# Column tiles for the token tails, and scores in two row-tiled groups behind a fence

## The chip, the cores and the metric

The kernel runs on one core of a Trainium2 chip. Its engines: TensorE (PE, its weight loads PEld) for matmuls, VectorE (DVE), ScalarE (ACT) and GpSimd (POOL) for the rest; PSUM is the memory, in banks, that the matmuls write. The metric is the device time in microseconds (us), a median of several executions; the spans in the profiles are some 1.8 us shorter.

## The reference

Eight batches of 576 tokens. First attention over pooled keys and values: keys and values are averaged over 8 neighbours (72 remain), 8 heads of 64. Then a mixer over tokens and one over channels:

```python
scores = scale * np.matmul(q, k_p.transpose(0, 1, 3, 2))      # per batch and head: 576 x 72
attn = softmax(scores);  x = attn @ v_p                        # 576 x 512 per batch, heads side by side
h = np.maximum(x.T @ w_tok1, 0.0) @ w_tok2                     # token mixer, 576 -> 256 -> 576
u = x + h.T
out = u + np.maximum(u @ w_ch1, 0.0) @ w_ch2                   # channel mixer, 512 -> 1536 -> 512
```

## The kernel before

All batches share one stream of instructions. The two excerpts below are abridged. "Unit n" is the channel mixer of batch n (lines 512 and 534, 24 steps each of two 128x512 matmuls). Step plans, one dictionary per unit, insert the other stages between these steps: `>s0` at step 22 is the first score stage of batch n+2.

576 tokens are 4 x 128 and a tail of 64. The tails of two batches are joined to a ninth "tile" of 128 rows and go through the channel mixer in a last unit, the tail unit. The second token-mixer stage for a joined tail took four full matmuls, with weights padded with zeros, so that each batch's tail falls in its own half of the rows:

```python
if c < 4:
    mms = [(w_tok2[:, m, c * P:(c + 1) * P], st["AT"][:, m, :]) for m in range(2)]
else:                                                   # u4: w_tok2t is half zeros
    mms = [(w_tok2t[:, m, half, :], tails[b // 2, half][:, m, :]) for half in range(2) for m in range(2)]
for i, (w, a) in enumerate(mms):
    nc.tensor.matmul(out=ps, lhsT=w, rhs=a, start=(i == 0), stop=(i == len(mms) - 1))
```

Scores contract over 64 dimensions, cut into two halves (`db`) of 32 rows, so four heads sit in the four 32-row groups of the array and run at once. A batch has two groups of four heads (`g`). It took three stages: `s0` and `s1`, the first 512 tokens of each group, and `s2`, the last 64 tokens of both:

```python
def score4(gs, n0, n):
    pss = [ps_two.tile([P, 2, 512], FP32) for _ in range(2)]         # four PSUM banks, one per row group
    for i, g in enumerate(gs):
        for db in range(2):
            for l in range(4):
                nc.tensor.matmul(out=pss[l // 2][0:SP, l % 2, i * n:(i + 1) * n], lhsT=kD[quad l, g, db],
                                 rhs=qD[quad l, g, db, n0:n0 + n], tile_position=(l * 32, 0), ...)
    # then two exponentials on ACT, PSUM -> ex
```

The kernel's PSUM pools take eight banks: four in `ps_two` (two buffers of two), three in `ps_one`, one in `ps_tr` ("pt").

The softmax here doesn't subtract the row's maximum and nothing guards it: scores larger than these inputs give would overflow.

## Time and profile before

| | |
|---|---|
| time | 275.05 us (274.76 to 275.32) |
| span of the profiled run | 272.9 us, granted clock 0.997 |
| TensorE busy | 97% |
| ACT, DVE, POOL busy | 40%, 52%, 48% |
| four-head score stage, 512 tokens, first start to next plain matmul | 0.56 us where it waits for nothing (eight of the ten in batches 3 to 7; the others 0.63 and 0.81) |
| tail score stage, 64 tokens, two groups | 0.26 us (four of the five in batches 3 to 7; the other 0.31) |
| tail's second stage | 0.86 us, four times |

How to read it: on a stream that is never idle, only the distance between starts tells what something costs.

### The profile page before, as it was taken

How to read it: one execution, taken by the hardware profiler on the slowest of the kernel's cores; microseconds unless marked ns; L12 is line 12 of the kernel's file. 1: busy time of each engine (PE TensorE's matmuls, PEld its weight loads, DVE VectorE, ACT ScalarE, POOL GpSimd, SP SyncE). 2: the span in 40 equal slices, each digit the busy share in tenths (PEclk: the TensorE clock that was granted, in tenths of full speed). 3: DMA queues.
4: the chain of work that ended last, by engine and by line, in shares of the span. 5: the costliest groups of instructions: out<-in, count | busy, mean ns of one | idle time of the engine just before them, and what ended most of it. 6: DMA issues, size and time to landing. Idle time of an engine off the chain costs nothing.

```text
span 272.9 us, 4515 instructions
## 1 busy us (share of the span) xinstructions
PE 265.5 (97%) x1812; PEld 129.5 (47%) x1812; DVE 142.8 (52%) x280; ACT 110.4 (40%) x182; POOL 131.2 (48%) x121
## 2 busy tenths in 40 slices
PE   8899999999999999999999999999999999999994
PEld 3774545544453544444445444544454444444443
DVE  5487777862674754776266627662765061022022
ACT  2443790058306535425632483147413603603600
POOL 8585221999996995998099999400000000000000
PEclk9999999999999999999999999999999999999998
DMA  7999999995649957993389463214223624024024
GB/s 140 199 202 206 206 205 208 207 202 97 101 63 164 208 107 157 172 211 107 79 144 220 129 115 74 62 59 118 59 58 96 130 58 103 0 57 99 2 49 105
DMA packets 40149, 33.99 MB, mean 125 GB/s; under 512 B 16960, under 2 KB 33600, under 8 KB 40128
## 3 DMA queue, kind: packets, MB, share of 16 engines
q0 software_dynamic: 18672, 17.64, 41.2%
q1 hardware_dynamic: 21296, 15.93, 23.5%
q8 instruction: 14, 0.23, 0.3%
q10 hardware_dynamic: 160, 0.13, 0.2%
q14 instruction: 7, 0.06, 0.1%
HBM read 38.86 MB, written 12.45 MB: 188 GB/s over the span
## 4 chain that ended last, share of the span: by engine, by line
PE 91%; ACT 3%; DMA 2%; DVE 2%; issue 1%; POOL 0%; POOLq 0%
PE p L534 33%; PE p L512 32%; PE p L410 6%; PE p L395 6%; PE p L344 3%; PE p L260 3%; DMA kr<-in_k_dram 2%; ACT ex L265 1%; ACT GT L516 1%; PE p L226 1%; PE p L546 1%; PE pt L420 1%; PE p L204 1%; PE pt L376 1%; PE p L461 0%
## 5 line engine op out<-in xcount | busy, mean ns | idle before, releaser
L534 PE MATMUL p<-w_ch,GT 128*128 128x512 bf16 x420 | 101.2, 379 | 0.0
L512 PE MATMUL p<-uT,w_ch 128*128 128x512 bf16 x384 | 92.4, 379 | 0.1
L516 ACT ACTIVATE GT<-p 128x512 bf16<-128x512 f32 x108 | 63.8, 598 | 70.3 <-PE p L512 69.9
L512 PEld LDWEIGHTS <-w_ch 128*128 128x128 bf16 x432 | 40.7, 98 | 48.2 <-issue 2.7
L534 PEld LDWEIGHTS <-GT 128*128 128x128 bf16 x420 | 38.0, 98 | 42.1 <-issue 3.1
L520 DVE TENSOR_TENSOR o<-p,u 128x512 f32<-128x512 f32 x32 | 21.9, 684 | 33.4 <-PE p L534 33.3
L265 ACT ACTIVATE ex<-p 72x1024 bf16<-72x1024 f32 (+1 forms) x42 | 31.7, 807 | 13.5 <-PE p L260 13.5
L147 POOL TENSOR_TENSOR t<-t 72x512 f32<-72x512 f32 x24 | 30.3, 1264 | 1.9
L146 POOL TENSOR_TENSOR t<-kr 72x1024 f32<-72x1024 bf16 x12 | 25.5, 2125 | 7.6 <-DMA kr<-in_k_dram 6.9
L411 DVE TENSOR_TENSOR u<-p,x 128x512 bf16<-128x512 f32 x32 | 21.6, 688 | 13.7 <-PE p L410 13.4
L146 POOL TENSOR_TENSOR t<-vr 72x1024 f32<-72x1024 bf16 x12 | 25.5, 2125 | 0.8
L442 DVE STREAM_TRANSPOSE uT<-v 128x512 bf16<-128x512 bf16 x20 | 13.0, 686 | 23.9 <-DMA v<-mem 23.9
L248 DVE STREAM_TRANSPOSE qD<-qb 128x576 bf16<-128x576 bf16 x28 | 20.6, 794 | 0.0
L362 DVE TENSOR_TENSOR x<-p,den 128x512 bf16<-128x512 f32 x28 | 19.4, 691 | 1.0
L410 PE MATMUL p<-AT,w_tok 128*128 128x512 bf16 x64 | 18.3, 379 | 0.2 <-ACT GT L516 0.2
L344 PEld LDWEIGHTS <-ex 72*128 72x128 bf16 x280 | 13.1, 98 | 8.3 <-DVE x L362 0.7
L386 ACT ACTIVATE AT<-p 128x512 bf16<-128x512 f32 x7 | 4.2, 597 | 30.7 <-PE p L395 30.7
L395 PE MATMUL p<-x,w_tok 128*128 128x512 bf16 x56 | 14.5, 379 | 0.0
L344 PE MATMUL p<-vp,ex 72*128 72x65 bf16 x280 | 14.3, 193 | 0.2 <-ACT ex L265 0.2
L356 DVE RECIPROCAL den<-p 128x8 f32<-128x8 f32 (+1 forms) x35 | 7.0, 200 | 13.3 <-PE p L344 13.0
L104 POOL DMA_DIRECT2D qb<-in_q_dram x7 | 5.2, 739 | 17.8 <-DVE qD L248 13.5
L260 PE MATMUL p<-qD,kD 32*72 32x512 bf16 (+1 forms) x224 | 11.7, 295 | 0.1
(105 smaller groups left out, 201.4 us busy)
## 6 DMA issues: line engine op xcount, KB each, us to landing
out_dram<-o SPq DMA_DIRECT2D x70, 128.0 KB, 2.4
kr<-in_k_dram POOLq DMA_DIRECT2D x7, 576.0 KB, 13.7
qb<-in_q_dram POOLq DMA_DIRECT2D x7, 576.0 KB, 6.3
vr<-in_v_dram POOLq DMA_DIRECT2D x7, 576.0 KB, 14.9
w_ch<-in_moe_w_ch_dram POOLq DMA_DIRECT2D x6, 512.0 KB, 13.8
mem<-u SPq DMA_DIRECT2D x10, 256.0 KB, 2.1
v<-mem SPq DMA_DIRECT2D x12, 160.0 KB, 3.7
v<-mem SPq DMA_DIRECT2D x8, 128.0 KB, 3.2
```

The lines of the kernel that those rows point to most:

```text
L146: eng.tensor_tensor(out=t4[:, 0:n], in0=t[:, hs, 0:4], in1=t[:, hs, 4:8], op=ALU.add)
L147: eng.tensor_tensor(out=t4[:, 0:n, 0:2], in0=t4[:, 0:n, 0:2], in1=t4[:, 0:n, 2:4], op=ALU.add)
L248: nc.vector.transpose(out=late("qD")[:, g, db].rearrange("m (r j u) -> m u r j", u=2, r=BR), in_=st["qraw"][:, g].rearrange("m (u r d) -> ...
L265: nc.scalar.activation(out=exv[:, a, :, gs.start:gs.stop, n0:n0 + n], in_=pss[a][0:SP, :, 0:len(gs) * n].rearrange("j l (g n) -> j l g n", ...
L344: nc.tensor.matmul(out=halves[h // 4][:, (h % 4) * (D + 1):(h % 4 + 1) * (D + 1)], lhsT=st["ex"][:, h * S + n0:h * S + n0 + P], rhs=st["vp ...
L395: nc.tensor.matmul(out=ps, lhsT=w_tok1[:, c if c < 4 else 4 + par, m * P:(m + 1) * P], rhs=st["x"][:, c, :] if c < 4 else st["xt"], start= ...
L410: nc.tensor.matmul(out=ps, lhsT=w, rhs=a, start=(i == 0), stop=(i == len(mms) - 1))
L411: nc.vector.tensor_tensor(out=dst, in0=ps, in1=x, op=ALU.add)
L512: nc.tensor.matmul(out=ps, lhsT=w_ch1[:, kk, m * P:(m + 1) * P], rhs=uT[:, kk, :], start=(kk == 0), stop=(kk == 3))
L516: nc.scalar.activation(out=GT[:, m, :], in_=ps, func=AF.Relu)
L520: nc.vector.tensor_tensor(out=o_sb, in0=ps, in1=(u_tails if n == B else st["u"])[:, c, :], op=ALU.add)
L534: nc.tensor.matmul(out=pss[c], lhsT=GT[:, m, c * P:(c + 1) * P], rhs=w_ch2[:, m, :], start=(m == 0), stop=(m == NM - 1))
```

## The change

Its intent is less TensorE time. (1) The tail's second stage uses two column tiles of 64, that is, two halves of the array's columns with a matmul each: the two batches' tails run at once, with no zeros. (2) For batches 3 to 7 the third score stage goes: each group of heads does its own 64 tail tokens within its visit to the row-tiled form. Two spare banks hold the tails, each shared by two row groups (0 and 2, 1 and 3), so a fence keeps groups 2 and 3 out until 0 and 1 have finished: a nop on ACT (an instruction that only waits and signals) that waits for the last early tail matmul (`done`), and on which the first late one waits. One such stage, in the form with four row groups, is called a visit or a group below. (3) All step plans are adapted.

```diff
+        def score9(g):
+            def go():
+                main = [ps_two.tile([P, 2, 512], FP32, name="p2") for _ in range(2)]
+                tail = [ps_tr.tile([P, 512], FP32, name="pt"), ps_one.tile([P, 512], FP32, name="p1")]
+                def mm(l, db, n0, n): ...      # tokens under 512: main bank of row group l; others: tail[l % 2]
+                full, rest = (0, 8 * BP), (8 * BP, BP)
+                for db in range(2):
+                    for l in (0, 1):
+                        done = mm(l, db, *rest)
+                    if db == 0:
+                        for l in (2, 3):
+                            mm(l, 0, *full)
+                fence = nc.scalar.nop()
+                tc.add_manual_dep(fence.ins, done.ins.name, ORDERED, ...)
+                for l, db in ((0, 0), (1, 0), (2, 1), (3, 1), (0, 1), (1, 1)):
+                    mm(l, db, *full)
+                for db in range(2):
+                    for l in (2, 3):
+                        again = mm(l, db, *rest)
+                        if (l, db) == (2, 0):
+                            tc.add_manual_dep(again.ins, fence.ins.name, ORDERED, ...)
+                # four exponentials: two of 72x1024 (main), then two of 72x128 (tails)
...
-                    mms = [(w_tok2t[:, m, half, :], tails[b // 2, half][:, m, :]) for half in range(2) for m in range(2)]
+                    for m in range(2):
+                        for half in range(2):
+                            nc.tensor.matmul(out=ps[half * BP:(half + 1) * BP], lhsT=w_tok2[:, m, 8 * BP:S],
+                                             rhs=tails[b // 2, half][:, m, :], start=(m == 0), stop=(m == 1),
+                                             tile_position=(0, half * BP))
... (w_tok2t, its memset and its two POOL copies removed; batches under 3 keep score4; plans, for example)
-    THIRD = {0: ">V0", 1: "s2 >K1", 3: "av1 >K0 >V1", ... 29: ">s0 lq4", 30: ">Q2 lk4", 33: ">s1", ...
+    THIRD = {0: "av1 >V0", 1: ">K1", 3: ">K0", ... 28: ">s0 lq4", 29: ">Q2", 32: ">s1 lk4", ...
```

## The prediction

> **What bounds the kernel now.** I read the page first: engine shares, slices, the chain that ended last.
>
> ```profile
> span 272.9 us, 4515 instructions
> PE 265.5 (97%) x1812; PEld 129.5 (47%) x1812; DVE 142.8 (52%) x280; ACT 110.4 (40%) x182; POOL 131.2 (48%) x121
> ...
> PEclk9999999999999999999999999999999999999998
> ...
> PE 91%; ACT 3%; DMA 2%; DVE 2%; issue 1%; POOL 0%; POOLq 0%
> ```
>
> TensorE is busy 97% of the span at the full granted clock, and 91% of the chain that ended last is TensorE. Busy does not mean that its time is well spent, so I went to the timeline of TensorE alone, around the tail work of batch 5 and the scores of batch 6 (columns: start, length, engine, line, operation, tiles, shape, count).
>
> ```profile
> 150.83 1.03 PE L410 MATMUL p<-AT,w_tok 128*128 128x512 bf16 x4
> 151.69 1.03 PE L410 MATMUL p<-AT,w_tok2t 128*128 128x512 bf16 x4
> 152.55 1.89 PE L512 MATMUL p<-uT,w_ch 128*128 128x512 bf16 x8
> ...
> 154.71 4.91 PE L512 MATMUL p<-uT,w_ch 128*128 128x512 bf16 x22
> 159.46 0.29 PE L195 MATMUL pt<-ident,kp 72*128 72x72 bf16 x4
> ...
> 160.55 0.63 PE L260 MATMUL p<-qD,kD 32*72 32x512 bf16 x8
> 161.11 0.61 PE L512 MATMUL p<-uT,w_ch 128*128 128x512 bf16 x2
> 161.55 1.89 PE L534 MATMUL p<-w_ch,GT 128*128 128x512 bf16 x8
> 163.37 0.63 PE L260 MATMUL p<-qD,kD 32*72 32x512 bf16 x8
> 163.93 3.63 PE L534 MATMUL p<-w_ch,GT 128*128 128x512 bf16 x16
> 167.49 0.33 PE L260 MATMUL p<-qD,kD 32*72 32x64 bf16 x16
> 167.75 1.04 PE L534 MATMUL p<-w_ch,GT 128*128 128x512 bf16 x4
> ```
>
> Read the starts, not the lengths (a length includes the pipeline's end, which overlaps the next matmul). From 154.71 to 159.46, 22 matmuls of 512 columns take 4.75 us: 0.216 us each. Eight plain ones before a score, 161.55 to 163.37, take 1.82 instead of 1.73: 0.09 is lost on entry. The score of 8 matmuls, 163.37 to 163.93, takes 0.56 where two rounds of four concurrent row tiles need 0.43: 0.13 is lost inside and on leaving. The tail score, 167.49 to 167.75, takes 0.26; less 0.13, its four rounds of 64 columns cost 0.034 each. The 16 plain matmuls after the score, 163.93 to 167.49, take 3.56 for 3.46, 0.09 of it the next entry: another 0.01. So **each visit to the row-tiled form costs about 0.23 us beyond its matmuls**, three times a batch. The tail's second stage takes four ordinary slots (151.69 to 152.55, 0.86 us), although half of each of its weight tiles is zeros.
>
> The waits come last. The longest waits of ACT and DVE are for TensorE. TensorE itself waits in few places; of those that the change touches, this one is visible in the timeline of all engines:
>
> ```profile
> 106.86 0.63 PE L260 MATMUL p<-qD,kD 32*72 32x512 bf16 x8
> ...
> 107.52 1.93 ACT L265 ACTIVATE ex<-p 72x1024 bf16<-72x1024 f32 x2 [1.02 <-PE p L260]
> ...
> 109.25 0.88 PE L260 MATMUL p<-qD,kD 32*72 32x512 bf16 x8
> ...
> 110.06 0.39 PE L534 MATMUL p<-w_ch,GT 128*128 128x512 bf16 x1
> ```
>
> Batch 4's second score takes 0.81 instead of 0.56: its second PSUM pair is free only when the exponentials end at 109.45. All such excesses over the ideal slots that I find after the first 23 us sum to about 1.9 us, so nothing but less TensorE work can gain much.
>
> **What the Trainium skill says.** (1) "TensorEngine Tiling (Array Packing)", Key Properties: changing the tiling mode drains TensorE, changing the tile does not. The trace agrees: 0.09 in, 0.13 inside and out, while the 72-row transposes at 159.46 (not tiled) cost 0.13 for four, with no extra. (2) "TensorE: Matmul & The Clock Gate", Part 3: matmuls in different row or column groups run concurrently; it gives 2.38x for three column tiles. For rows the trace agrees (eight in 0.56 us); no matmul of this kernel is column-tiled. (3) The tiling page, Restrictions and Gotchas: different row tiles must not write one PSUM bank at once. That is why the new score has a fence. (4) "PSUM — Partial Sum Buffer", Engine vs sequencer instructions: a nop runs on the sequencer, which waits for earlier instructions to be dispatched, not finished. The kernel before has no such nop, so the trace can't confirm that the fence passes a running activation.
>
> **The change part by part.**
> *Tail second stage* (u4 of batches 1, 3, 5, 7: four times). Four full slots, 0.863 us, become two rounds of two column tiles: 2 x 0.216 + 0.23 for a visit (assuming a column visit costs what a row visit does) = 0.66. Saved 0.20 x 4 = **0.80 us**, all on TensorE, so on the path. Its eviction on DVE stays one of 0.69 us.
> *Scores of batches 3 to 7.* Before, a batch pays 3 x 0.23 + 2 x 0.43 + 4 x 0.034 = 1.69 us. After, it pays two visits. In each, row groups 0 and 1 do two tail matmuls (0.034 each) and two full ones (0.216 each), groups 2 and 3 the same in the other order: 0.50 if the four groups run independently. 2 x (0.50 + 0.23) = 1.46. Saved 0.23 x 5 = **1.16 us**: nearly the third visit alone, since the tail matmuls still take their own columns on each row group.
> *The fence.* ACT's nop waits for the second tail matmul of group 1, which starts 0.04 to 0.06 after the visit's start. A 64-column matmul's record is 0.19 long, ACT starts about 0.035 after a matmul's end (last score matmul to exponential, single records), TensorE about 0.05 after ACT (the wait at 109.45 ended at 109.50). So the fence opens near 0.36 to 0.40, and the tails of groups 2 and 3 want to start near 0.45. I count 0.
> *Evictions.* Per batch ACT had four 72x1024 (1.02 us) and two 72x256 (0.39). The latter become four 72x128, some 0.27 each by the slope between the two sizes. ACT gains about 0.3 us per batch, off the path at 40%. But a group's tails are evicted last, near 0.72 + 0.92 + 0.92 + 0.27 = 2.8 us after its start, and one of them lives in the only buffer of the pool "pt", which the second group's first matmul needs. Batch 4's second score now comes four steps (1.73 us) after the 0.72 us of the first: at 2.45. It waits some 0.43 where it waited 0.25: **+0.18 us**. Batch 3's two scores are five steps apart (2.88): near 0. The plans of batches 5 to 7 leave six or seven steps: 0.
> *Plan of unit 2.* The third score of batch 3 is gone and its first attention product moves to step 0, about 2.45 after the second score; the exponentials of the main columns end near 2.66: **+0.2 us**.
> *Removed set-up.* Two POOL copies (0.6 us) and one DVE memset (0.27) leave the head. POOL and DVE are not what the head waits for there: 0.
> *Other moves.* The waits near 39, 44, 58 and 78 us (about 0.9 us in all) belong to plans that hardly move, so I keep them.
> Sum: -0.80 - 1.16 + 0.18 + 0.20 = -1.58: 273.5; the shortened waits that a retuned plan probably brings I put at -0.1: **273.4 us**.
>
> **Rivals.**
> *Ordered ends.* The clock-gate page also says that matmuls start and end strictly in program order. If a tail matmul behind a full one in another row group cannot finish before it, a group costs three rounds of 0.216 plus tails, near 0.65 to 0.70, and the score's gain falls to zero or -0.7 us in all: about 274.5. The starts in this trace are 3 ns apart in order, but all concurrent matmuls have equal length, so it can't tell.
> *Fence behind ACT's queue.* If the nop waits for a running activation to finish, it can be late by up to 0.4 us where a 0.6 us relu or the earlier exponentials run. In ten groups that could be 1 to 3 us: 274.5 to 276. Against: the skill's page; most groups stand where ACT has no relu.
> *Column tiles don't overlap* (weight loads without the fast mode, which the tiling page says column tiling disables; two moving streams): the tail stage becomes 1.1 us instead of 0.86, so 0.8 is lost and +0.9 paid: 275.1 with the rest as above. For row tiles, 72-column loads without trouble at 0.034 us speak against.
> *Better than thought.* The new plans also remove most of the 1.9 us of waits: near 272.
>
> **Range and chances.** All parts of the gain are TensorE time on the path; the full saving without any new wait is 1.96 us (273.1). Half of it lost gives 274.1. I take 272.4 to 274.7. A gain of 2% would be 5.5 us, more than saving and all waits together (3.9): 0.01. A loss of 2% would need ten fences of 0.5 us: 0.02.
>
> **What would show it.** In the timeline of TensorE after: score groups of 16 matmuls taking 0.62 to 0.64 from first start to the next plain matmul, 0.09 before them, twice per batch from batch 3; about 0.78 would be the ordered ends, 0.9 and more a late fence (a wait of TensorE for ACT within the group). The tail stage at 0.57 plus 0.09 instead of 0.86. Waits for the exponentials before batch 4's second group and batch 3's first attention product. The prediction is wrong if TensorE's slots around the visits are as told but the sum still differs: then a wait that I don't see has moved.

## The result

The changed kernel takes 274.14 us (273.74 to 274.35), the kernel before 275.03 in the same rounds: ratio 0.9968, interval [0.9955, 0.9981]. A ratio is the mean time of one kernel's runs over that of the other's of the same rounds, so it is not quite the ratio of the medians. Two later timings of the same kernel gave 0.9994 and 0.9976 (told below). All of them are inside 2%; the interval of the second, [0.9972, 1.0015], includes 1, and that the gain is there is read from the stretch defined next.

The head of the kernel, where the first loads land, starts the steady stream at times that differ by about a microsecond between executions. So beside the times I use a stretch of the trace that does not contain it: from the start of batch 1's second score stage to the first matmul of the tail unit. It is 212.41 us before (35.76 to 248.17) and 211.68 after (35.73 to 247.41), and came out as 211.68 or 211.69 in all three profiles of the changed kernel. So **0.73 us** were won in the stream.

The page after:

```profile
span 272.2 us, 4534 instructions
PE 264.5 (97%) x1812; PEld 129.6 (48%) x1812; DVE 141.9 (52%) x279; ACT 110.9 (41%) x192; POOL 130.4 (48%) x119
...
PE 89%; ACT 3%; DMA 3%; DVE 2%; POOL 1%; issue 1%; POOLq 0%
```

Nothing has changed its place: TensorE still sets the time. Next the timeline of TensorE after, at batch 5's tail stage:

```profile
150.99 0.59 PE L440 MATMUL p<-AT,w_tok 128*128 128x512 bf16 x2
151.51 0.62 PE L446 MATMUL p<-AT,w_tok 128*64 128x512 bf16 x4
152.07 2.76 PE L553 MATMUL p<-uT,w_ch 128*128 128x512 bf16 x12
```

The two matmuls before take 0.52 (0.43 and 0.09 of entry), the tail stage 151.51 to 152.07, or 0.555 by the single records: 0.66 with the entry and the 0.01 after it, in place of 0.86. That is the predicted 0.66.

Then one score group, batch 7's first, in the timeline of all engines:

```profile
187.34 0.21 PE L276 MATMUL pt<-qD,kD 32*72 32x64 bf16 x1
187.34 0.41 PE L276 MATMUL p<-qD,kD 32*72 32x64 bf16 x3
187.40 0.19 PE L276 MATMUL pt<-qD,kD 32*72 32x64 bf16 x1
187.40 0.63 PE L276 MATMUL p<-qD,kD 32*72 32x64 bf16 x7
187.45 0.60 ACT L557 ACTIVATE GT<-p 128x512 bf16<-128x512 f32 x1 [0.27 <-PE p L553]
187.87 0.14 PEld L276 LDWEIGHTS <-kD 32*72 32x72 bf16 x4 [0.32 <-ACTq L286]
187.88 0.21 PE L276 MATMUL pt<-qD,kD 32*72 32x64 bf16 x1
...
188.06 0.11 PEld L553 LDWEIGHTS <-w_ch 128*128 128x128 bf16 x2
188.06 0.39 PE L553 MATMUL p<-uT,w_ch 128*128 128x512 bf16 x1
```

(A merged line shows the shape of its first matmul; the x3 and x7 contain full ones.) From 187.34 to 188.06 the group takes 0.72 us; 0.62 to 0.64 was predicted. The weight load of the late tails waits for "ACTq L286", which is the nop, and starts only at 187.87, 0.53 after the group's start. The nop's own record is at 187.81, in the middle of the 0.60 us relu that ACT runs from 187.45: it does not wait for a running activation. In the list of waits this is a new line, nine times of ten groups (us in total, times, longest):

```profile
PEld L276 <- ACTq L286: 2.9, 9, 0.3
```

Most of that idle time of the weight loader is harmless, since the full matmuls run meanwhile; what counts is that the tails start at 0.536 after the group's start and not near 0.45 (single records), and that they then follow each other at 0.056 and not 0.034, as their weight loads, too, came only after the fence.

The two other places of interest. First, batch 3's second group and what stands before it on DVE:

```profile
84.68 0.81 DVE L246 STREAM_TRANSPOSE qD<-qb 128x576 bf16<-128x576 bf16 x1
...
85.26 0.21 PE L276 MATMUL pt<-qD,kD 32*72 32x64 bf16 x1
...
85.55 0.18 PE L276 MATMUL pt<-qD,kD 32*72 32x64 bf16 x1
...
86.14 0.60 PE L575 MATMUL p<-w_ch,GT 128*128 128x512 bf16 x2
```

It takes 0.88 us. Its second tail starts 0.29 after the first instead of 0.056: it reads the second half (`db` 1) of the queries, and DVE ends transposing that half at 85.49. Second, batch 4's second group and batch 3's first attention product:

```profile
108.85 0.27 ACT L299 ACTIVATE ex<-pt 72x128 bf16<-72x128 f32 x1
...
109.17 0.18 PE L276 MATMUL pt<-qD,kD 32*72 32x64 bf16 x1 [0.26 <-ACT ex L299]
```

```profile
87.16 1.01 ACT L297 ACTIVATE ex<-p 72x1024 bf16<-72x1024 f32 x1
...
87.87 0.59 PE L378 MATMUL p<-vp,ex 72*128 72x65 bf16 x8
...
88.30 0.38 PE L553 MATMUL p<-uT,w_ch 128*128 128x512 bf16 x1
```

The group waits 0.33 us for the tail bank, which the exponential frees at 109.12. The attention product takes 0.43 instead of 0.26 because the last main exponential ends at 88.17.

The sum over the stream, from these distances (each visit with 0.103 for entry and after):

| | before | after | difference |
|---|---|---|---|
| tail stage, 4 times | 0.86 each | 0.66 each | -0.83 |
| scores of batches 3 to 7 | 10 x 0.663 + 5 x 0.365 = 8.46 | 10 x 0.825 = 8.25 | -0.21 |
| waits at batches 3's and 4's scores | 0.07 + 0.25 + 0.05 | 0.15 + 0.33 | +0.11 |
| batch 3's first attention product | 0 | 0.17 | +0.17 |
| a wait near 49 us (second tail-plan stage of unit 0) | 0 | 0.08 | +0.08 |
| batch 4's first attention product (112.72 before) | 0.08 | 0 | -0.08 |
| sum | | | -0.76 (trace: -0.73) |

### The profile page after: what moved, and what is told of

The parts are those of the page before. It is cut to its first block, busy times and chain, and to the rows that moved or that the text cites. A ratio compares the mean times of both kernels' runs of the same rounds, so it can differ in the third digit from the quotient of the medians.

```text
span 272.2 us, 4534 instructions
## 1 busy us (share of the span) xinstructions
PE 264.5 (97%) x1812; PEld 129.6 (48%) x1812; DVE 141.9 (52%) x279; ACT 110.9 (41%) x192; POOL 130.4 (48%) x119
## 4 chain that ended last, share of the span: by engine, by line
PE 89%; ACT 3%; DMA 3%; DVE 2%; POOL 1%; issue 1%; POOLq 0%
PE p L553 33%; PE p L575 32%; PE p L429 6%; PE p L440 5%; PE p L378 3%; DMA vr<-in_v_dram 3%; PE p L276 2%; ACT ex L263 1%; ACT GT L557 1%; PE p L224 1%; PE p L587 1%; PE pt L276 1%; PE p L446 1%; PE pt L458 1%; ACT ex L297 1%
## 5 line engine op out<-in xcount | busy, mean ns | idle before, releaser
L575 PE MATMUL p<-w_ch,GT 128*128 128x512 bf16 x420 | 100.1, 379 | 0.0
L297 ACT ACTIVATE ex<-p 72x1024 bf16<-72x1024 f32 x20 | 19.3, 1015 | 8.9 <-PE p L276 8.9
L429 PEld LDWEIGHTS <-w_tok 128*128 128x128 bf16 x70 | 6.8, 98 | 8.4 <-issue 0.3
L86 POOL DMA_DIRECT2D vr<-in_v_dram x10 | 7.7, 773 | 6.3 <-PE p L553 3.3
```

Of the source, the lines that this page charges most:

```text
L297: nc.scalar.activation(out=exv[:, a, :, 0:8 * BP], in_=main[a][0:SP], func=AF.Exp, scale=scale)
L429: nc.tensor.matmul(out=ps, lhsT=w_tok1[:, c if c < 4 else 4 + par, m * P:(m + 1) * P], rhs=st["x"][:, c, :] if c < 4 else st["xt"], start= ...
L575: nc.tensor.matmul(out=pss[c], lhsT=GT[:, m, c * P:(c + 1) * P], rhs=w_ch2[:, m, :], start=(m == 0), stop=(m == NM - 1))
```

## The experiments

"Stretch" is the one defined above. Hypotheses: the fence is late because a matmul's completion is reported in program order; against it, that the hop through ACT is slow by itself, or that the late tails are late for another reason. And: the tail stage gives nearly all of the gain; against it, that both halves give.

### The halves alone

`only_tail`: the kernel before with the diff's tail stage only, old scores and plans. `only_score`: the changed kernel with the old tail stage put back.

```diff
 only_score (the changed kernel, then)
-                    for m in range(2): for half in range(2): matmul(... tile_position=(0, half * BP))
+                    mms = [(w_tok2t[:, m, half, :], tails[b // 2, half][:, m, :]) ...]   # four full matmuls
```

> The kernel before with the column-tiled tail stage alone, old scores and old plans. Theory A (the tail stage gives nearly all of the gain): four visits of 0.66 us in place of 0.86, so 0.82 us less than before, about 274.2, as fast as the whole change. Theory B (both parts gain, as the prediction had it, and waits of the new plans eat some of it): the tail stage gives some 0.4 to 0.5 us of the 0.9, about 274.6.

> The changed kernel with the old tail stage (four full matmuls, zero-padded weights): new scores and new plans alone. Theory A: the scores' own gain (10 visits of 0.82 in place of 15 that sum to 8.4 us: 0.2 us) goes into the new waits before batch 3's and 4's second groups and first attention product: within 0.3 us of before, 274.8 to 275.1. Theory B: 0.4 to 0.5 us faster than before, about 274.6.

| | time | ratio to before | stretch |
|---|---|---|---|
| only_tail | 273.85 (273.15 to 274.16) | 0.9963 [0.9949, 0.9978] | 211.75 |
| only_score | 274.94 (274.37 to 275.56) | 1.0006 [0.9990, 1.0022] | 212.49 |

Theory A holds: the tail stage alone is as fast as the whole change; the new scores with their plans alone are 0.08 us slower in the stretch (-0.21 of visits, +0.28 of waits by the table; its two rows of 0.08 cancel). The tail stage's stretch is 0.66 shorter and not 0.83: three of its four visits gave their 0.21 (the drift between the two traces grows by that at each), while in unit 0 0.14 came back as a wait before the transposes near 54 us, under the old plan.

### The order before the fence

`early_tails`, all four early tails first. The result stays right.

```diff
                 for db in range(2):
                     for l in (0, 1):
                         done = mm(l, db, *rest)
-                    if db == 0:
-                        for l in (2, 3):
-                            mm(l, 0, *full)
+                for l in (2, 3):
+                    mm(l, 0, *full)
```

> The changed kernel with one reordering: in each new score group all four tail matmuls of row groups 0 and 1 are issued before the first full matmuls of groups 2 and 3, instead of around them. Theory of ordered completion (the fence is late because the tail matmul it waits for reports only when the full matmuls issued before it have ended): ACT's nop comes near 0.30 us after the group's start instead of 0.47, the late tails start near 0.49 instead of 0.54 and follow each other in 0.034, the group takes about 0.65 us instead of 0.72, ten times: about 0.7 us less than the changed kernel, 273.5. Rival (the hop through ACT has a fixed cost of 0.41 us after the matmul's start): nop near 0.47, the late tails no earlier, the group 0.72 to 0.75: 274.1 to 274.4.

Measured: 273.23 us (273.02 to 274.20), ratio 0.9947 [0.9932, 0.9961]; stretch 210.94, 0.74 less than the changed kernel. In its timeline, batch 5's second group:

```profile
136.66 0.59 PEld L276 LDWEIGHTS <-kD 32*72 32x72 bf16 x16 [0.42 <-DVE o L560]
...
137.13 0.19 PE L276 MATMUL pt<-qD,kD 32*72 32x64 bf16 x1
...
137.29 0.60 PE L574 MATMUL p<-w_ch,GT 128*128 128x512 bf16 x2
```

The merged line of sixteen weight loads hides a pause of 0.149 us, too short for the view to break the line: by the single records the late tails' first load still waits for the nop, but it starts 0.36 after the group's start, where it started at 0.53. So it is in time while the full matmuls run; the late tails start at 0.47, as they do without any fence (below), and the group takes 0.63. The nop's record (single records) stands 0.29 us after the group's start in nine groups, where it stood at 0.47 in nine of the changed kernel; the tenth of both is batch 3's second group, which waits for its queries.

`split_fulls` changes the dose instead: the first full matmuls of groups 2 and 3 are cut in two.

```diff
  (in place of the same three lines; go_on=1 keeps the second half from starting its sum anew)
+                    for l in (2, 3):
+                        mm(l, 0, db * 4 * BP, 4 * BP, go_on=db)     # 256 columns before, 256 after the second tails
```

> Right result. The changed kernel with the first full matmuls of row groups 2 and 3 cut into two of 256 columns: the first halves stay before the second tails, the second halves come right after them. Ordered completion: the nop follows the end of the last matmul before the tail it waits for, 0.11 us earlier than with 512 columns, so it comes near 0.36 us after the group's start (0.47 in the changed kernel, 0.29 in the reordered one). A fixed cost of the hop: 0.47 again. A cost of having other row groups streaming at all: 0.47.

Measured, one look with a correct result: the nop at 0.361 in the nine groups that wait for nothing else, a group 0.626 us, stretch 210.92. Its single time (276.62) is not used: its granted clock was 0.985, lower in the head (tenths 7 in two slices), and its stream began about 3 us later. Batch 5's second group:

```profile
139.96 0.26 PEld L276 LDWEIGHTS <-kD 32*72 32x72 bf16 x14 [0.42 <-DVE o L560]
...
140.39 0.15 PEld L276 LDWEIGHTS <-kD 32*72 32x72 bf16 x4 [0.17 <-ACTq L285]
```

Three doses, one rule (single records, us after the group's start):

| matmul that ends last among those up to the fence's | its end | nop |
|---|---|---|
| changed: full matmul of row group 3, 512 columns | 0.010 + 0.402 = 0.41 | 0.47 |
| split_fulls: its first 256 columns | 0.01 + 0.30 = 0.31 | 0.36 |
| early_tails: the awaited tail matmul itself | 0.059 + 0.194 = 0.25 | 0.29 |

The awaited tail matmul starts at 0.06 in all three, and its own record ends at 0.25 in all three; full matmuls of groups 2 and 3 run beside it in all three. It is also the one that increments the semaphore on which the nop waits; the next increment comes with a matmul whose record ends at 0.69, after every nop, so a coarser semaphore is not the cause. So neither the hop through ACT nor the presence of other row groups is what is slow: **its completion is seen only when the matmuls issued before it have ended**, and the hop then takes some 0.05 us. (Ends in the trace are modelled; the nop's time and the next starts are not.)

### No fence at all

`no_fence`, a wrong result (the comparison with the reference passed it all the same, which says nothing for it, and little for the tails of the other runs: their correctness rests on the code):

```diff
-                    dst = ... else tail[l % 2][0:SP, l // 2 * BP:(l // 2 + 1) * BP]
+                    dst = ... else (tail[l] if l < 2 else main[1][:, l % 2])[0:SP, 0:BP]
-                fence = nc.scalar.nop()  (and both dependencies)
-                in_=tail[l][0:SP, 0:2 * BP]...          +  in_=tail[l][0:SP, 0:BP], read twice
```

> Wrong result on purpose: in each new score group the tails of row groups 2 and 3 go into their own main banks instead of the shared tail banks, so that no fence is needed and there is none; the tail exponentials read the tails of groups 0 and 1 twice. Same matmuls, order and exponentials otherwise. If the fence is what makes the group 0.09 us longer than predicted, the group takes 0.62 to 0.64 us and the kernel 0.8 to 0.9 us less than the changed one, about 273.3. If the late tails are late for another reason (order of issue, weight loads), the group stays at 0.70 or more and the time at 274.0 or more.

Measured: 273.63 us (273.37 to 274.03), ratio 0.9959 [0.9946, 0.9972]; stretch 210.90; a group 0.624 (137.24 to 137.86 for batch 5's second). The fence costs 0.78 us of the stretch: 0.098 in eight of the ten groups, while the second groups of batches 3 and 4 wait for something else in its place. `early_tails` gets 0.74 of it back with the fence in place. The time misses the expected 273.3 by 0.3; the intervals of this kernel and of `early_tails` overlap, and the profiled execution's stream began 0.6 us later, so I don't read a difference out of it.

### The waits that remain

`early_plan` adds three moves of the plan to `early_tails`:

```diff
-    SECOND: 43: ">Q3"       THIRD: 0: "av1 >V0", 1: ">K1"     32: ">s1 lk4", 33: "T0"
+    SECOND: 41: ">Q3"       THIRD: 0: ">V0", 1: "av1 >K1"     32: "lk4", 33: ">s1 T0"
```

`q3_early` is the changed kernel with the first of them alone; `changed_again` the changed kernel unaltered.

> The changed kernel itself, unaltered, as a control beside the others: 274.1, some 0.9 us less than before.

> The reordered groups (all early tails first) with three moves of the plan against the three waits that remain: batch 3's last query transposition two steps earlier (its second group waits 0.25 us for it), batch 4's second group one step later (0.42 us for the tail bank), batch 3's first attention product one step later (0.17 us for the exponentials). If these waits are on the path, up to 0.75 us less than the reordered kernel, about 272.6 (1.6 less than the changed one). Rival (a wait moved is a wait given back to the next consumer): less than 0.3 us, 273.0 or more.

> The changed kernel with batch 3's last query transposition two steps earlier, nothing else. If batch 3's second group is 0.88 us long because its second-half tails, which now come 0.06 us after the group's start and not 0.24, wait for that transposition on DVE, the group falls to 0.72 us like the others. If it waits for a PSUM buffer and the exponentials of the first group, it stays above 0.85.

| | time | ratio to before | stretch |
|---|---|---|---|
| changed_again | 274.54 (273.43 to 275.39) | 0.9994 [0.9972, 1.0015] | 211.69 |
| early_plan | 272.56 (272.16 to 273.23) | 0.9926 [0.9910, 0.9941] | 210.40 |
| q3_early | 274.47 (one run) | - | 211.67 |

The control's stretch is the same to 0.01 while its times spread over 2 us: what varies is the head. `early_plan` won 0.54 of 0.75. `q3_early` was a miss of mine: batch 3's second group stayed at 0.88, but by the expectation's own words that would have meant a PSUM wait, and it doesn't. Steps 41 and 43 both lie behind the "store" of the third output tile (the add on line 561 that ends it; step 41's matmuls complete its input). In the trace of `q3_early` the transposition still follows that add on DVE (84.55, then 85.15). `q3_before_store` has it at step 40:

```diff
-              43: ">Q3"
+              40: ">Q3"
```

> The changed kernel with batch 3's last query transposition three steps earlier, so that on DVE it now stands before the store of the third output tile and not behind it (the first try left DVE's order as it was and so showed nothing). If batch 3's second group waits for this transposition, the group falls from 0.88 to 0.72 us, and the stretch from batch 1's second group to the tail unit from 211.68 to about 211.5 us. If it waits for the first group's PSUM buffers, it stays at 0.85 or more, or the wait moves ahead of the group.

Its timeline of DVE alone:

```profile
81.23 2.17 DVE L246 STREAM_TRANSPOSE qD<-qb 128x576 bf16<-128x576 bf16 x3
84.17 0.69 DVE L561 TENSOR_TENSOR o<-p,u 128x512 f32<-128x512 f32 x1 [0.77 <-PE p L575]
```

Now three transpositions run before the store, in time in which DVE was idle. The group takes 0.72, the stretch is 211.43, 0.25 less than the changed kernel; time 273.41 (272.98 to 273.83), ratio 0.9946 [0.9922, 0.9971]. The wait was for the transposition.

`early_plan_2` is `early_plan` with step 40, and two further moves (batch 2's `s0` from step 3 to 4, batch 1's `av0 av1` from 26, 27 to 27, 28). `early_plan_3` is the same without those two. With it ran the changed kernel a third time.

> The reordered groups with the plan's moves of before (the transposition now ahead of the store), and two more: batch 2's first group one step later (it waits 0.26 us for a transposition) and batch 1's first two attention products one step later (0.32 us for exponentials). If each wait is on the path, the stretch from batch 1's second group to the tail unit shrinks from 210.40 us (first plan) by 0.24 for the transposition, 0.26 and up to 0.32 to about 209.6, and the time to about 271.9; if the later steps give them back, no change from the first plan, 272.6.

> The reordered groups with three moves only: the transposition ahead of the store, batch 4's second group one step later, batch 3's first attention product one step later; without the two moves that gave their time back. The stretch from batch 1's second group to the tail unit should be the first plan's 210.40 less the transposition's 0.24, about 210.15 us; the time about 272.4, less than both the kernel before and the changed one.

> The changed kernel once more, because its two timings differ (ratios 0.9968 and 0.9994): if the head's start varies from run to run, the time lies between 274.0 and 274.6 and the stretch from batch 1's second group to the tail unit is again 211.68 us.

| | time | ratio to before | stretch |
|---|---|---|---|
| early_plan_2 | 272.92 (272.32 to 273.62) | 0.9936 [0.9915, 0.9957] | 210.25 |
| early_plan_3 | 272.52 (272.11 to 272.67) | 0.9916 [0.9897, 0.9934] | 210.16 |
| changed_third | 274.13 (273.76 to 274.59) | 0.9976 [0.9957, 0.9996] | 211.68 |

The transposition gave its 0.24 and the two extra moves gave nothing (210.25 against 210.16 without them): with batch 2's first group later, the wait at it (0.26) is gone, and its second group takes 0.81 instead of 0.56. `early_plan_3` beats both kernels: 2.25 us of the stretch below before, 1.52 below the changed one.

## Why the prediction was right or wrong

The time was inside the range: 274.14 against 273.4 and 272.4 to 274.7, 0.7 us too optimistic. In the stretch, where all of the forecast 1.68 us lies, 0.73 was won: short by 0.95, and one step made that. That the times differ by 0.9 and not by 0.73 is the varying head, so luck. So is part of the range's success: it allowed for half of the saving to be lost, while the step that lost it was counted at 0.

- *Tail second stage, -0.80.* Right: 0.66 each, -0.83 by the visits. The assumption that a column visit costs what a row visit does held to the hundredth. That it is worth about the whole gain was not foreseen.
- *Scores, -1.16 (0.23 x 5 is 1.15).* Wrong in size, -0.21. The work of a group was right: without a fence it takes 0.624 us where I said 0.63. What failed is **"The fence. ... I count 0"**: it makes a group 0.098 us longer (0.722 against 0.624), and the stretch 0.78. I had it open 0.36 to 0.40 after the start by adding the tail matmul's own 0.19 us to its start (the terms that I gave sum to 0.32 to 0.34; `early_tails`, where they do apply, has the weight load at 0.36). The three doses show that its completion waits for the full matmuls issued before it, so the nop came at 0.47, the late tails were 0.07 late and their weight loads, behind the same wait, were not hidden: 0.03 more.
- *The rivals.* "Ordered ends" named the right property and drew the wrong consequence. Row groups do start their next matmul before an earlier one in another group has ended (0.091 after the start, beside a full matmul that ends at 0.41), so the group was not three rounds; but the semaphore is ordered. "Fence behind ACT's queue" fell with the nop at 187.81. "Column tiles don't overlap" fell with 0.555 us for two pairs.
- *Evictions and plan, +0.18 and +0.20.* Right in place. Batch 4's second group waits 0.33 us for the tail bank (I said 0.43) where it waited 0.25: +0.08; batch 3's attention product +0.17. "Batch 3's two scores ... near 0" was wrong: 0.15, and it is not a PSUM buffer but the transposition of the second query half, which the new order needs 0.06 us into the group and not 0.24. `q3_before_store` shows it.
- *Other moves.* The waits near 39, 44, 58 and 78 us stayed, as said; a new one of 0.08 came near 49. The -0.1 for a better plan did not come.
- *Set-up.* The head's variation between executions is larger than any effect of the removed copies and memset; left open.

## What to carry to other kernels

When a semaphore is to fire early, put the matmul that fires it before the long ones, not merely beside them on another part of the array: moving two short matmuls of a group ahead of two long ones won as much (0.74 us of the stretch) as the whole rewrite (0.73). Where a stage is reordered, ask again when each of its inputs is needed, and whether a step moved in a plan passes the instruction that its engine really waits behind. And measure a stream of 212 us from landmark to landmark when the head varies by a microsecond.

## What the Trainium skill lacked or had wrong

- "TensorEngine Tiling (Array Packing)", Key Properties, says that changing the mode drains TensorE but not what it costs. Here: 0.09 us before the first matmul, and some 0.12 to 0.13 inside and on leaving (0.56 for two rounds of 0.216), the same for four row tiles (0.560) and two column tiles (0.555).
- "TensorE: Matmul & The Clock Gate", Part 3, says that matmuls end in program order and draws from it that one increment on the last one is enough. It does not draw the other side: a short matmul's increment is held back by longer ones issued before it in other row groups (nop at 0.47, 0.36 and 0.29 us with 512, 256 and no such columns issued before it), while the array itself goes on (next full matmul of the same row group at 0.091).
- The tiling page, Restrictions, says that column tiling disables the fast weight load, but not what that costs. The 64-column loads took 0.106 to 0.109 us by their records against 0.098 for 128 columns, but the second round of column tiles starts 0.240 after the first, as the second round of row tiles does (0.243).
- "PSUM — Partial Sum Buffer", Engine vs sequencer instructions, is confirmed for a nop on ACT (record at 187.81 within an activation from 187.45 to 188.05). No page gives the hop from a matmul over ACT to a weight load: 0.04 to 0.06 us from the matmul's modelled end to the nop, 0.07 from the nop to the weight load that waits for it.
